# One Strassen level in layer 1 of the last two token groups, with a new instruction order

## The chip, the cores and the metric

The kernel runs on one core of one Trainium2 chip. The metric is the device time of one execution in microseconds; lower is better. Where a kernel was run several times, the median is given. The engines of the core are named as in the profile: PE is the matrix engine (TensorE), PEld its weight loads, DVE is VectorE, ACT is ScalarE, POOL or G is GpSimd, and SP is SyncE, which here only issues DMA transfers.

## The reference

The reference is a linear attention followed by a two-layer network with a gate. In the kernel's terms there are 8 batches of 576 tokens, 8 heads of 64, a model width of 512 and a hidden width of 2048.

```python
def _attn_ref(q, k, v):                      # each (8, 8, 576, 64)
    pos = np.arange(S); theta = np.pi / 2 * pos / S
    phi = lambda x: concat([relu(x) * cos(theta), relu(x) * sin(theta)], -1)
    kv  = einsum('bhsf,bhsd->bhfd', phi(k), v)
    z   = sum(phi(k), axis=2)
    num = einsum('bhsf,bhfd->bhsd', phi(q), kv)
    den = einsum('bhsf,bhf->bhs', phi(q), z)[..., None] + 1e-06
    return num / den

def _moe_ref(x, w_in, w_out):                # x (4608, 512), w_in (512, 2048), w_out (2048, 512)
    h = x @ w_in                             # "layer 1"
    g = h * np.cos(h)                        # the gate
    return g @ w_out                         # "layer 2"
```

The result of the attention, with heads side by side, is `x`.

## The kernel before

The tokens of a batch are split into 4 tiles of 128 tokens and a rest of 64. The four tiles of batch `b` form token group `b` (512 tokens); the rests of all batches form the group `"r"`. The groups are worked on in the order `GO`, and layer 1 of a group is laid beside layer 2 of the one before it.

```python
GO = [0, 1, 2, 3, 4, 5, 6, "r", 7]
STR = set()            # groups whose layer 1 uses a Strassen level: none
AT = {"r", 7}
```

Every piece of work is an operation of a plan: it names the engines that may do it (A for ACT, V for DVE, G for GpSimd), what it depends on and which buffers it takes and frees. A list of numbers, `ORDER`, found by a search outside of the kernel, gives the order in which the operations are emitted and the engine of each (`40A` is operation 40 on ACT). As each engine works through its own instructions in that order, `ORDER` settles everything that happens on it.

The parts of the plan for a batch: loads of k, q, v (SyncE); the features `phi` (ACT, DVE or GpSimd); a copy of v to 16 bit; the transposes of the query features (on PE for batches 0 and 1, by DMA after that); KV products; N products (numerator and denominator); reciprocal and ratio (DVE); the transpose of `x` (on PE for batches 0 to 2, by DMA after that).

```python
def feat(eng, b, name, t, g, hs=ALLH):                    # L201 to L212
    ...
    if eng == "A":
        nc.scalar.activation(out=dst, in_=src, func=AF.Relu, scale=sc)
    else:
        (nc.vector if eng == "V" else nc.gpsimd).tensor_scalar(
            out=dst, in0=src, scalar1=0.0, scalar2=sc, op0=ALU.max, op1=ALU.mult)
...
RING = {"m1": 4, "l2": 2, "at": 1, ..., "qp": 4, "x16": 3, "ch": 3, "g": 2, "s": 3, "ld": 2, "p5": 3, ...}
```

`RING` gives the number of buffers of each kind: `m1`, `l2` and `at` are PSUM, `x16` holds the ratio of a token tile until its transpose has landed.

Layer 1 of a group, plain form: for each of 16 blocks of the hidden width, 4 matmuls of 512 columns into one PSUM buffer, then the sine on ACT and the product with it on DVE.

```python
def moe1(key, g, js, cs, s0, s1):                         # L319 is its matmul
    ...
    for n, j in enumerate(js):
        for c in cs:
            nc.tensor.matmul(ps[key][:, n, :], lhsT=w_in_sb[:, c, j * P:(j + 1) * P],
                             rhs=x[:, c, s0:s1], ...)
def sin(key): ...     # ACT, L381: sin(h + pi/2) from PSUM to "ch"
def gate(eng, key, dst): ...   # DVE: g = h * ch, read from PSUM
```

Layer 2 is in Strassen's form for all groups (seven products X, Y, Z of half-size blocks instead of eight, with sums of `g` and of the weights made on DVE, and additions from PSUM on DVE). The same form for layer 1 stands in the code, but no group uses it as `STR` is empty. Three of the four sums of `w_in` that it needs (`w_in_sum`, tile `WS`) are made all the same.

```python
def quad(g, qd, n):                                       # a quarter of the hidden width, product n of 7
    a11, a12, s3, a22 = (w_in_block(k_, e) for e in range(2) for k_ in range(2))
    ...
    bank, first, lhs, rhs = (
        ("X", True, a11, x_block(g, 0, 0)), ("Z", True, ws[0], xs[0]),
        ("Y", False, ws[1], xs[1]), ("X", False, a12, x_block(g, 1, 0)),
        ("Y", False, s3, x_block(g, 0, 1)), ("Z", False, ws[2], x_block(g, 1, 1)),
        ("Y", False, a22, xs[2]))[n]
    ...
    for i in range(2):
        for c in range(2):                                # 4 matmuls of 256 columns
            nc.tensor.matmul(ps[(g, qd, bank)][:, i, :], lhsT=lhs[:, c, 2 * qd + i, :], rhs=rhs[:, c, :], ...)
...
def quads(g, base, ga):                                   # used for the groups in STR
    for n in range(4): x_sum(...)                         # DVE: sums of x, once a group
    for qd in range(4):
        p1 = mm(0, ...)                                   # X
        p5 = mm(1, ...)                                   # Z
        y1 = op({"A": 0.6, "V": 0.69}, EV, y_seed, deps=[p1, p5], ...)   # copies X into Y
        e5 = op({"A": 0.6, "V": 0.69}, EV, evac5, deps=[p5, ga], ...)    # copies Z out of PSUM
        p6 = mm(2, [xsum[1], wsum1[1], y1], ...)          # onto Y
        p2 = mm(3, [y1], ...)                             # onto X, then sine and gate
        z1 = op({"V": 0.69}, EV, z_add, deps=[p6, e5])    # Z = Y + copy
        p7 = mm(4, [xsum[2], s3_done(), z1], ...)         # onto Y
        c = op({"V": 0.69}, EV, c22, deps=[p7])           # a fourth result, then sine and gate
        p3 = mm(5, [wsum1[2], z1], ...)                   # onto Z, then sine and gate
        p4 = mm(6, [xsum[3], c], ...)                     # onto Y, then sine and gate
...
def cover():                                              # L298: two matmuls of 512 columns with a zero weight
    t = ppool.tile([P, 2, 512], F32, name="cover", tag="at", bufs=1)
    for n in range(2):
        nc.tensor.matmul(t[:, n, :], lhsT=zero, rhs=w_in_sb[:, 0, 0:512], start=True, stop=True)
```

Of the kernel before, what the change touches and what calls it, by code (L numbers as in the profile page):

```python
# [44 lines left out]


ORDER = """
115 22 25 230 180 184 883 818 24 229 342 21 40A 41V 42A 60 43V 44A 61V 62 45A 63V 64 38A 32V 36V
39A 70 37V 31A 34V 51G 53A 54G 52V 35V 50A 4G 30A 33V 5G 46V 57A 71 47V 9G 48A 72V 66 7G 49A 58V
75 56V 85 59A 76V 68 11G 77V 55A 69A 15G 86V 73 87V 78 227 13G 74V 79A 88 89V 90 65A 80 91V 17G  # L50
120 81V 82V 116 19G 67A 92V 95 83 96V 100 84A 97V 93 94V 98 105 101V 99A 117 102V 121 118A 106V
103 132 107V 122A 133 119V 104A 110 134A 136 123V 128 135V 129 124 130A 111V 112V 125 137 126A
131V 140 138A 127V 108 141 109A 139V 113 142A 144 114V 145 143V 152 146A 231 164 147V 153 233
165 154A 168 166A 155V 148 149 167V 176 150A 188V 177 156 151V 178A 199 179V 172 190V 169 189V
160 170A 173 171V 157 174A 161 191V 158A 343 200 162A 159V 236 201A 192V 202 175V 238 163V 203
181V 204A 241 185V 261A 210 182V 263A 211 193V 243 262A 207 186V 246 212A 264V 265A 208 887 248
183V 258A 283 940 209V 254A 281 213V 273G 272A 194V 282A 274G 214 275G 187V 271G 257A 277G 205V
215 259A 279G 251V 280G 217 255A 252V 276G 278G 196V 253A 256A 284V 260A 216V 267A 291 197V 222
292A 269A 305 206V 295 293 266A 296V 218 340 306V 294A 297V 270A 310 195V 285 268A 289 307V 286A
344 223 198V 346 219A 315 891 287 316V 224A 220G 317V 290A 311V 320 349 321V 225G 312V 288A 318  # L60
335 322V 300 419 336V 323 351 319A 301V 308 302V 324A 313 314A 298 309V 303 299V 304A 325 330
326V 819 501 327V 369A 835 331V 328 820 332V 329A 371G 836 821A 370V 831 837A 822V 384 333 832
334A 838V 827 833A 372G 859 354 373V 828 834V 374A 860 843 337V 861A 823 829A 375G 386 844 862V
824 845A 830V 338 825A 356 339V 875 826V 388 376A 876 863 846V 877A 851 361G 368V 390 366A 852
878V 855 853A 856 363V 377A 847 367V 364G 864 857A 362V 848 865A 858V 948 359A 866V 867 849A
365G 854V 839 360A 868 850V 871 869A 884V 840 381A 879 382G 870V 880 841A 379G 885V 958 383A
380G 842V 881A 872 378A 394 886V 420 873A 395 882V 392 949 396A 417 874V 421 397 888V 950A 423
398A 951 889V 399V 952 890V 402 953A 956 426 955V 403A 959 944 404V 957 428 960A 954V 407 1024
961V 405 408A 400 406V 431 962 446A 401V 409V 963 448A 447G 433 412 450A 964V 410 965 449V 413A
411A 414V 451G 970 461 452A 443V 415 453A 971 416V 463 441A 438V 895 439G 442V 444A 440V 465 901  # L70
896A 437V 445V 458A 904 459G 467 897V 457A 966 456G 436V 460A 972V 919 905A 975 967V 902A 973G
471 920A 903V 907 968G 454A 906V 472 908A 455V 928 499 473A 909V 503 474 921V 929A 469 910 475A
930V 922 911A 505 476V 931 923A 912V 477 479 932A 924V 892 480A 933V 916 893A 481V 508 898 917A
894V 482 484 899A 934 918V 485A 900V 925 935A 486V 510 1032 926A 936V 487 489 913 490A 927V 528G
1033 491V 914A 513 937 915V 1034A 492 941V 1035 938A 502 530G 529A 939V 515 494 942V 578 660 543
1036 945V 1040 1037A 532G 946V 524A 1042 522V 525A 1041 1038V 1028 518A 531G 947V 1043 533A 495V
496V 982 534A 1108 1044A 1003 1039V 535G 545 983A 1045V 991 538A 984V 547 542A 976 521V 540G
992A 985 943V 497 536G 977A 993V 1049 549 1004A 539A 1005V 1009 986A 978V 537G 979 1010A 987V
519A 1046 1011V 980A 527V 988 526G 541A 580 981V 1021 989A 582 520V 990V 551 1050 1022A 523G
1023V 997 1051V 1000 998A 999V 994 1052G 1001A 585 1002V 587 1012 995A 996V 1047 1013A 1025V  # L80
605A 1018 590 1048V 607A 606G 1006 1014V 1019A 1054 608V 1007A 1020V 609A 1116 1008V 610A 1015
611V 1026V 1055 1016A 579 592 612A 1017V 1117 1059 1056A 1027V 553 1118A 1057G 1029V 554 1030V
1119 555A 576 596G 599A 1031V 556 1120 620 595A 557V 558V 1124 1121A 597G 1123V 559 598A 561
1126 562V 622 600A 563V 1127 1112 602A 619G 1122V 564 604A 566 616G 1125 567V 624 568V 1128A
617G 601A 1192 615G 1129V 571 569 572A 618A 573V 1130 626 613A 1133 603V 574 614V 630 628 1131
631 662 1132V 1134 632A 658 664 633 1135V 1138 634A 635V 1136G 1096 667 638 1097A 1105 639V 636
640V 1139 1106A 669 1098V 643 641 1140A 1143 1107V 1078 1141G 644V 1066 645V 1079A 687G 1093
1080V 1067A 646 1068V 648 1094A 1060 672 649A 1095V 1072 1061A 689G 650V 688A 1069 1062V 651
1073A 653 1070A 674 1074V 1084 691G 737 690A 702 1071V 1200 654A 1085A 655V 1102 704 679A 680G
1086V 684A 1087 678V 656 1103A 692V 1063 1088A 1104V 706 685G 1090 1064A 1089V 681A 1099 1065V  # L90
1091A 682V 1075 686G 1100A 1092V 677A 1081 1101V 1076A 1165 661 1113V 1082A 683G 1144 1077V
1166A 1114V 699A 1159 698A 1167V 1201 697G 1145A 1083V 693G 700A 1147 1202V 1160A 1109V 1183
1148A 1161V 701A 1203 1110V 1184A 1168 695A 1185V 1208 1149V 696A 1162 1111V 1169A 710 694A
1170V 712 1163A 1146V 708 1153 1164V 713 1154A 739 1115V 1209 714A 735 741 1155V 715 1204 716V
717V 1150 1205A 1206V 718 1210 1151A 1207V 744 720 1196 1152V 1171 746 721V 722V 1180 1172A 1211
1173V 1181A 723 1182V 764A 725 1276 749 1189 726V 1212A 765G 727V 1177 1190A 1213V 728 730 1178A
1156 766V 751 731A 767V 1214 779 1157A 732V 756A 763G 1217 759V 733 758A 1215 762V 781 757A 755V
1218 1216V 754G 761A 1174 1191V 1219A 1158V 760A 1222 1175A 1193V 1220G 1284 775A 1176V 1223
774G 778A 1194V 777A 776G 1186 1227 1195V 1237 768V 1187A 738 1224V 769A 1264 1188V 1225G 1238A
783 789 1179V 1265A 1285 770A 1239V 1231 1286V 771G 1266V 1255 1232A 1197V 1249 1256A 1198V 772G  # L100
785 1228 1250A 1199V 790 1251V 1287 791A 1233V 773A 1267 1257V 1229A 787 1246 1268A 1230V 1258
1247A 1269V 1248V 1270 1259A 1260V 1240 1271A 1272V 1234 1241A 1242V 792 1235A 1288 793V 794V
1273 1289A 1290V 795 1294 1274A 1291V 797 1295 1236V 798A 1275V 1243 799V 1292 1244A 1296V 800
802 1280 1293 803A 1245V 1252 1297V 1360 1277V 1301 1253A 804V 1298 1254V 805 807 1299 808A
1278V 1302 1300V 1279V 1306 1303A 809V 1304G 1368 810 1307 812 1308V 1311 1369 813A 1309G 814V
1261 1370A 815 1371 1262A 1263V 1376 1281V 1372 1282V 1423 1373A 1374V 1377 1283V 1411 1375V
1378 1327 1364 1336 1328A 1329V 1379 1337A 1338V 1342 1380A 1444 1381V 1318 1343A 1344V 1385
1319A 1320V 1348 1354 1349A 1350V 1386 1355A 1356V 1330 1387A 1388G 1324 1331A 1332V 1382 1325A
1326V 1315 1312 1316A 1317V 1383 1313A 1314V 1321 1384V 1452 1322A 1323V 1390 1357 1351 1358A
1359V 1391 1352A 1353V 1402 1395 1412A 1392V 1424A 1417 1413V 1403A 1393G 1453 1404V 1418A 1426  # L110
1454A 1419V 1425V 1339 1427A 1428V 1429 1340A 1341V 1333 1430A 1431V 1441 1334A 1335V 1396 1442A
1443V 1455 1397A 1361V 1414 1398V 1345 1415A 1362V 1405 1346A 1416V 1347V 1460 1406A 1363V 1456
1407V 1420 1457A 1458V 1399 1421A 1365V 1422V 1432 1400A 1401V 1462 1433A 1366V 1438 1448 1367V
1461 1439A 1459V 1463 1440V 1408 1464V 1465V 1435 1409A 1410V 1469 1436A 1445V 1466 1437V 1489
1446V 1467 1447V 1470 1468V 1434V 1474 1471A 1449V 1472G 1479 1450V 1475 1451V 1480 1476A 1477G
1490 1481V 1487 1491A 1482 1488 1483 1492V 1493 1485V 1484V 1496 1486V 1494 1497 1495V 1501
1498V 1502 1499 1506 1503A 1507 1504 817 1508A 1505 1509 1510
"""


@with_exitstack
def kernel(
    ctx: ExitStack,
    tc: tile.TileContext,
    q: bass.AP,
    k: bass.AP,
# [557 lines left out]

    GO = [0, 1, 2, 3, 4, 5, 6, "r", 7]
    ALONE = (1, 7)
    STR = set()
    AT = {"r", 7}
    WSUM = {"Vp": 1.24}
    XSUM = {"Vp": 0.43}  # L690
# [37 lines left out]
    def layer1(g, base, after):  # L728
# [3 lines left out]
        gate_ops[g] = {}  # L732
        if g in STR:
            quads(g, base, ga)
# [258 lines left out]
```

## Time and profile before

| | |
|---|---|
| time, median of 3 runs | 313.49 us (312.3 to 313.61) |
| span of the profiled run | 310.2 us |
| DMA | 53.30 MB, mean 172 GB/s |
| granted PE clock, mean | 0.987 |

The costliest groups of instructions on the page (busy us, and the mean of one):

| what | count | busy us | mean ns |
|---|---|---|---|
| PE, layer 1 (L319, xT) | 640 | 122.3 | 338 |
| ACT, sines (L381) | 144 | 84.3 | 596 |
| DVE, gates (L332, g) | 128 | 84.8 | 685 |
| GpSimd, features of q (L211) | 20 | 42.0 | 2106 |
| ACT, features of q (L209) | 44 | 29.9 | 713 |
| DVE, ratio (L276) | 44 | 26.2 | 594 |

How to read it: a line of code can be that of a helper which records many kinds of work, so groups are told apart by their tiles. M is a PSUM tile of layer 1, PX, SD and PZ are those of layer 2, `ch` is the sine, `N` the attention's numerator and denominator. Matmuls overlap, and so do instructions of DVE and ACT that follow each other; the mean of one is longer than the step from one to the next. The chain of waits is followed back from the last instruction, each step to what released it.

### The profile page before, as it was taken

The numbers are of one execution on the slowest core, as the hardware profiler recorded it, in microseconds if no ns is written. First come the engines' busy times: TensorE is split into PE (matmuls) and PEld (weight loads), VectorE is DVE, ScalarE is ACT, GpSimd is POOL, SyncE is SP. The second block draws the span as 40 slices with busy tenths as digits, with TensorE's granted clock in tenths as the row PEclk, the third lists the DMA queues.
The fourth block names the chain that finished last, engine by engine and source line by source line (L and its number), as shares of the span: only waits on it lengthen the run. The fifth ranks groups of instructions, "written<-read, shape, count | busy, mean of one in ns | idle before, by whom it ended". The sixth has DMA issues, their size and how long they took to land.

```text
span 310.2 us, 6724 instructions
## 1 busy us (share of the span) xinstructions
PE 281.8 (91%) x2615; PEld 205.1 (66%) x2615; DVE 233.6 (75%) x440; ACT 180.3 (58%) x326; POOL 111.7 (36%) x114
## 2 busy tenths in 40 slices
PE   8758958889999998999987699999999999999993
PEld 8647837768887556558863346675578766566882
DVE  1867767979988888888844698898887665788741
ACT  2776428988847857867726388586731254654200
POOL 1270004058708329983714990276001101100220
PEclk9999979999999999999999799999999999999999
DMA  7799993099899999899899983999314401100123
GB/s 220 244 145 200 209 343 109 0 288 288 155 266 279 232 278 256 172 257 357 149 161 312 294 118 59 264 294 215 70 34 73 117 2 68 68 2 0 50 87 136
DMA packets 77247, 53.30 MB, mean 172 GB/s; under 512 B 46112, under 2 KB 74784, under 8 KB 77216
## 3 DMA queue, kind: packets, MB, share of 16 engines
q1 hardware_dynamic: 69920, 39.86, 53.3%
q0 software_dynamic: 6848, 12.59, 16.0%
q8 instruction: 20, 0.33, 0.5%
q10 hardware_dynamic: 448, 0.44, 0.4%
q14 instruction: 11, 0.09, 0.1%
HBM read 36.74 MB, written 9.44 MB: 149 GB/s over the span
## 4 chain that ended last, share of the span: by engine, by line
PE 60%; DMA 20%; ACT 6%; DVE 3%; issue 1%; SPq 1%; POOL 0%; ACTq 0%; DVEq 0%
PE M L319 29%; PE SD L430 11%; PE PX L430 9%; DMA xT<-x 9%; DMA w_out_sb<-in_moe_w_out_dram 7%; PE PZ L430 7%; PE KV L247 3%; ACT kp L209 3%; DMA km<-in_k_dram 2%; DMA qm<-in_q_dram 2%; PE N L256 1%; ACT qp L209 1%; DVE g L332 1%; DVE x L276 1%; ACT ch L381 1%
## 5 line engine op out<-in xcount | busy, mean ns | idle before, releaser
L319 PE MATMUL M<-xT,w_in_sb 128*128 128x512 f16 (+1 forms) x640 | 122.3, 338 | 6.0 <-DMA xT<-x 1.8
L381 ACT ACTIVATE ch<-M 128x512 f32<-128x512 f32 x144 | 84.3, 596 | 57.0 <-PE M L319 55.4
L319 PEld LDWEIGHTS <-w_in_sb 128*128 128x128 f16 x704 | 67.2, 98 | 52.5 <-issue 5.3
L332 DVE TENSOR_TENSOR g<-M,ch 128x512 f16<-128x512 f32 x128 | 84.8, 685 | 14.2 <-ACT ch L381 12.8
L430 PEld LDWEIGHTS <-g 128*128 128x128 f16 x640 | 61.9, 99 | 20.4 <-issue 7.3
L211 POOL TENSOR_SCALAR qp<-qm,CS 128x512 f16<-128x512 f32 x20 | 42.0, 2106 | 40.7 <-DMA qm<-in_q_dram 22.8
L430 PE MATMUL PX<-w_out_sb,g 128*128 128x256 f16 x256 | 34.4, 280 | 4.1 <-DMA w_out_sb<-in_moe_w_out_dram 3.0
L465 POOL DMA_DIRECT2D out_dram<-ost x14 | 7.8, 560 | 76.2 <-ACT ost L189 55.2
L209 ACT ACTIVATE qp<-qm,CS 128x512 f16<-128x512 f32 x44 | 29.9, 713 | 6.9 <-DMA qm<-in_q_dram 6.9
L276 DVE TENSOR_TENSOR x<-N,rec 128x512 f16<-128x512 f32 (+1 forms) x44 | 26.2, 594 | 8.6 <-DMA xT<-x 6.4
L211 POOL TENSOR_SCALAR kp<-km,CS 128x512 f16<-128x512 f32 x14 | 29.3, 2105 | 3.1 <-DMA km<-in_k_dram 2.7
L430 PEld LDWEIGHTS <-s 128*128 128x128 f16 x256 | 24.5, 98 | 4.7 <-issue 0.2
L209 ACT ACTIVATE kp<-km,CS 128x512 f16<-128x512 f32 x37 | 24.5, 711 | 2.5 <-DMA km<-in_k_dram 2.5
L191 POOL CAST V<-vm 128x512 f16<-128x512 f32 (+1 forms) x24 | 12.6, 563 | 28.3 <-DMA vm<-in_v_dram 27.8
L332 DVE TENSOR_TENSOR gr<-M,ch 128x512 f16<-128x512 f32 x16 | 11.1, 692 | 10.2 <-ACT ch L381 10.2
L211 DVE TENSOR_SCALAR kp<-km,CS 128x512 f16<-128x512 f32 x29 | 16.3, 597 | 2.1 <-DMA km<-in_k_dram 2.1
L430 PE MATMUL PZ<-w_out_sb,g 128*128 128x256 f16 x128 | 16.6, 273 | 0.0
L430 PE MATMUL PZ<-WT,s 128*128 128x256 f16 x128 | 16.3, 273 | 0.0
L319 PE MATMUL M<-xR,w_in_sb 128*128 128x512 f16 x64 | 15.5, 379 | 0.0
L430 PE MATMUL SD<-WT,g 128*128 128x256 f16 x112 | 14.5, 273 | 0.7 <-ACT ost L189 0.7
L256 PEld LDWEIGHTS <-qT 128*128 128x128 f16 x256 | 12.5, 98 | 3.8 <-issue 0.9
L256 PE MATMUL N<-kvz,qT 128*128 128x65 f16 x256 | 14.1, 194 | 1.0 <-DVE x L276 0.9
(91 smaller groups left out, 312.2 us busy)
## 6 DMA issues: line engine op xcount, KB each, us to landing
out_dram<-ost POOLq DMA_DIRECT2D x28, 256.0 KB, 4.5
qm<-in_q_dram SPq DMA_DIRECT2D x8, 640.0 KB, 5.5
km<-in_k_dram SPq DMA_DIRECT2D x8, 640.0 KB, 8.0
qm<-in_q_dram SPq DMA_DIRECT2D x8, 512.0 KB, 6.0
km<-in_k_dram SPq DMA_DIRECT2D x8, 512.0 KB, 8.4
vm<-in_v_dram SPq DMA_DIRECT2D x6, 640.0 KB, 6.7
vm<-in_v_dram SPq DMA_DIRECT2D x6, 512.0 KB, 6.2
w_in_sb<-in_moe_w_in_dram POOLq DMA_DIRECT2D x4, 512.0 KB, 9.1
```

The lines of the kernel that those rows point to most:

```text
L191: (nc.vector if eng == "V" else nc.gpsimd).tensor_copy(out=out, in_=in_)
L209: nc.scalar.activation(out=dst, in_=src, func=AF.Relu, scale=sc)
L211: (nc.vector if eng == "V" else nc.gpsimd).tensor_scalar(out=dst, in0=src, scalar1=0.0, scalar2=sc, op0=ALU.max, op1=ALU.mult)
L247: nc.tensor.matmul(tile_[:, n, hh, :], lhsT=kps[b][:, t, h].rearrange("p g d -> p (g d)"), rhs=V1[:, t, h, :], start=(t == 0), stop=(t == NT))
L256: nc.tensor.matmul(tile_[:, n, hh, :], lhsT=qT(p, t)[:, h, :], rhs=kvzs[p][:, h, :], start=(i == 0), stop=(i == len(parts) - 1))
L276: nc.vector.tensor_tensor(out=dst, in0=tile_[:, :, :, 0:D], in1=rec.unsqueeze(3).broadcast_to((P, nb, HB, D)), op=ALU.mult)
L319: nc.tensor.matmul(ps[key][:, n, :], lhsT=w_in_sb[:, c, j * P:(j + 1) * P], rhs=x[:, c, s0:s1], start=(c == 0 and n == 0), stop=(c == NCT ...
L332: (nc.vector if eng == "V" else nc.gpsimd).tensor_tensor(out=out, in0=in0, in1=in1, op=op)
L381: nc.scalar.activation(out=ps[("ch", key)], in_=ps[key].rearrange("p j s -> p (j s)"), func=AF.Sin, bias=math.pi / 2.0, scale=1.0)
L430: nc.tensor.matmul(ps[(g, bank)][:, i, :], lhsT=lhs[:, j, i * P:(i + 1) * P], rhs=rhs[:, c * HJ // 2 + j], start=(first and i == 0 and j = ...
L465: e0.dma_start(out=five[:, t0:t0 + 2, :], in_=blocks(ost, n))
```

## The change

Layer 1 of the groups `"r"` and 7, the last two, takes the Strassen form that stands in the code. This is to save one of eight products in the part of the kernel in which PE has hardly a pause. With it comes another searched order for the whole kernel; as the Strassen form adds operations, the numbers in the two lists stand for different operations from that part on, and other operations go to other engines too. In neither order does GpSimd run an operation with two inputs; it copies, makes features and issues DMA transfers.

```diff
@@ ORDER @@
-115 22 25 230 180 184 883 818 24 229 342 21 40A 41V 42A 60 43V 44A 61V 62 45A 63V 64 38A 32V 36V
... (all lines of the list are replaced)
+180 24 184 22 25 230 229 342 883 115 818 21 40V 42V 41A 43V 44A 60 62 61V 46A 63V 48A 32V 37A
...
     GO = [0, 1, 2, 3, 4, 5, 6, "r", 7]
     ALONE = (1, 7)
-    STR = set()
+    STR = {"r", 7}
     AT = {"r", 7}
```

What the new order holds, counted by kind:

| operations | before | after |
|---|---|---|
| plain products of layer 1 on PE / with sine and gate | 176 / 144 | 144 / 112 |
| Strassen products of layer 1 on PE / sines and gates of them | 0 / 0 | 56 / 32 |
| seeds of Y and copies of Z in layer 1 (ACT, DVE) | 0, 0 | 15, 1 |
| z additions and c22 additions in layer 1 (DVE) | 0 | 16 |
| sums of x, fourth sum of w_in (DVE) | 0, 0 | 8, 1 |
| features of q on ACT, DVE, GpSimd | 44, 16, 20 | 35, 24, 21 |
| features of k on ACT, DVE, GpSimd | 37, 29, 14 | 38, 29, 13 |
| copies of layer 2's results and seeds on ACT, DVE | 30, 14 | 41, 3 |

The "cover" matmuls stand at the end of PE's sequence before, and ahead of the second Strassen product of group `"r"` after. The transposes of `x` of batch 5 stand among the loads of batch 6 in SyncE's sequence, before as "load q, load q, load k, transpose 0, load k, transpose 1, transpose 2", after as "load q, load q, transpose 0, load k, transpose 1, load k, transpose 2". The first features of query 2 on ACT and DVE stand before the first sine and gate of group 1 before, and behind the first ones after.

## The prediction

> **What bounds the kernel now.** I read the busy shares of the page first, then the busy time by stretch, then the chain of waits, and last the waits of single stretches. The busy shares (engine, busy us, share of the span, instructions) make TensorE (PE) the engine to look at, with VectorE (DVE) second.
>
> ```profile
> PE 281.8 (91%) x2615; PEld 205.1 (66%) x2615; DVE 233.6 (75%) x440; ACT 180.3 (58%) x326; POOL 111.7 (36%) x114
> ```
>
> An average hides the stages, so the next view is busy time by stretch. Columns: stretch and its length, then busy us and instruction count of PE, weight loads, DVE, ACT and POOL, then the granted PE clock, the share of the DMA engines and GB/s.
>
> ```profile
> 0.00:43.00 43.00, 32.47 (x397) 28.52 (x398) 26.33 (x66) 23.04 (x41) 9.08 (x22) 1.00 0.98 216
> 43.00:72.00 29.00, 24.85 (x289) 20.47 (x287) 24.93 (x58) 22.53 (x41) 9.58 (x16) 0.94 0.54 180
> 72.00:147.00 75.00, 72.99 (x694) 52.65 (x693) 66.30 (x118) 54.63 (x102) 45.68 (x32) 1.00 1.03 249
> 147.00:177.00 30.00, 23.64 (x245) 16.77 (x243) 17.78 (x39) 14.50 (x29) 16.66 (x15) 0.94 0.97 226
> 177.00:240.00 63.00, 62.56 (x538) 41.82 (x537) 54.57 (x96) 39.78 (x72) 22.98 (x18) 1.00 0.64 144
> 240.00:305.00 65.00, 64.34 (x457) 44.50 (x456) 43.74 (x68) 25.40 (x44) 7.66 (x14) 1.00 0.16 50
> ```
>
> The reader is to see two kinds of stage. In 72–147 and from 177 on PE is busy 97 to 99%: there a microsecond of PE work less is a microsecond less, unless the products begin to wait. In 0–72 and in 147–177 PE has holes, and the clock column falls to 0.94 in two of these stretches. The chain of waits (start, length, what) says what the holes are:
>
> ```profile
> 20.63 22.09 DMA w_out_sb<-in_moe_w_out_dram
> ...
> 61.85 5.71 DMA qm<-in_q_dram
> 67.67 0.72 ACT qp L209
> 68.66 0.97 ACT ch L381 x2
> ...
> 162.75 9.69 DMA xT<-x
> 172.57 0.70 DVE x L276
> 173.31 1.06 PE N L256 x16
> ```
>
> So until 42.8 us the second weight matrix is awaited. Near 62–68 ACT stands at a feature of batch 2 whose query load has not landed. At 162.75 a DMA transpose of x (batch 5, token tile 0) is issued and lands 9.7 us later; the normalised tile that reuses its buffer waits for it, and PE waits for that:
>
> ```profile
> PE N L256 <- DVE x L276: 5.2, 2, 4.7
> ```
>
> **What the Trainium skill says.** "TensorE: Matmul & The Clock Gate", section "Back-to-back issue gap", gives N/2.4 + 2.5 ns for a warm matmul of N columns: 216 ns at 512 and 109 ns at 256. The trace agrees: four 512-column matmuls take 0.86 us in the chain, eight of 256 columns 0.87. The same page, "What's actually happening", has the array drop to half clock after about 3.4 us of idleness and recover after a busy window of about that length. The trace agrees here too: a wait of 3.00 us before 42.8 and one of 4.75 us before 173.3 are each followed by 3.4 us at clock 0.5, which costs about 1.7 us more. "VectorE: DVE Perf Modes", "The perf-mode tier table", caps tensor_tensor at double rate for 16-bit SBUF operands and at single rate with PSUM: the trace has 0.68–0.69 us both for 1024 fp16 elements and for 512 elements read from PSUM. "DMA: Bandwidth & Descriptors", "Queues, rings and completion order", says that on each DMA engine the descriptors of one ring are consumed in ring order; the 9.69 us transpose, issued behind 1.8 MB of loads from the same SyncE queue, fits.
>
> **The change, part by part.**
>
> (a) Layer 1 of the groups r and 7. Before, each needs 16 x 4 matmuls of 512 columns: 64 x 0.216 = 13.8 us. After, each needs 4 quads x 7 products x 4 matmuls of 256 columns: 112 x 0.109 = 12.2 us. Saved: 1.6 us a group, 3.3 us in all. Weight loads rise from 64 to 112 a group at 98 ns; that is under the 109 ns of a 256-column matmul, as layer 2 has it already without a visible loss. Both groups are in the last stage, where PE is 99% busy, so this counts in full if nothing new waits.
>
> (b) The two "cover" matmuls of 512 columns, 0.43 us, stood behind the last product (305.35 us, beside the last output copy, which cost nothing). They now stand ahead of the second product of group r: plus 0.4 us. Net on PE: about -2.9 us.
>
> (c) DVE in the last stage. New there: 8 z additions and 8 c22 additions (0.69–0.70 us each, as the like additions of layer 2), one evacuation 0.69, the fourth sum of w_in 1.2 (like its three sisters at 1.22), and 8 sums of x of 512 fp16 elements, which I estimate at 0.4 from the 0.68 of 1024 elements. That is 11.7 + 1.2 + 3.2 = 16.1 us; three copies of layer 2 go from DVE to ACT, -2.1. The 32 gates are the same in number and size. DVE goes from 43.7 to about 58 us of busy time in some 62. That looks full, but busy times overlap: gates that follow each other start 0.60–0.61 us apart though each is 0.69 long, so 58 busy is about 51 of engine time, 82%.
>
> (d) ACT in that stage. 8 seeds of Y and 7 evacuations at 0.60, plus 1.8 for the copies from DVE: 25.4 + 10.8 = 36 us of 62. No bound.
>
> (e) Chains. In a quad the first product must pass through ACT (seed), product 6, DVE (z), product 7, DVE (c22) before product 4: about 0.6 + 0.7 + 0.7 on the engines, three products of 0.435 and the hand-overs, some 4.5 us. The new PE order puts two to three quads and products of layer 2 between, so each quad has about 7 us of other PE work around it. I allow 0.7 us for stalls. Tail: -2.2 us.
>
> (f) The searched order elsewhere. PE's own sequence before group r is nearly the same. Three places differ where the trace shows a wait. First, at 62–68 us ACT and DVE stood at features of query 2 ahead of a copy of x and ahead of the first gates of group 1; these features now come after several sines and gates, and the third one went to GpSimd, which is idle there. PE had about 2.7 us of holes in 60–70; I count -1. Second, near 160 SyncE issued two query loads and a key load ahead of the transpose that landed after 9.7 us; now two query loads alone, 1.15 instead of 1.8 MB. At the 226 GB/s of that stretch the missing 0.64 MB are 2.8 us, and ten instead of nine products of PE stand between the five N blocks of batch 5. The wait of 4.75 us could shrink to about 1 and its half-clock window go. Against that, ACT now has the features of query 6 after four sines of group 4 instead of after six, and the last query feature of batch 5, which frees the buffer for that load, is late on GpSimd (2.1 us each there, against 0.71 on ACT). I count -2, not -5. Third, new places where an in-order queue stands at a late load must be expected in an order whose search knew no real landing times: +1.
>
> Sum: 313.5 - 2.2 - 1 - 2 + 1 = 309.3; I say **309.5**.
>
> **Rivals.** *DVE becomes the bound of the tail.* For it: DVE gets the largest share of the new work, and a z addition behind a gate that waits for a sine holds up two products. Against it: 18% of engine time is left, and DVE already sits idle there for 10.2 us of group r's gates, waiting for sines. It would eat the 3.3 us and perhaps 3 more: 313 to 317. *The gain is given back in the middle.* The order before 240 us is a different one, and a single new wait of over 3 us at a load costs that and a half-clock window: 312 to 316. *The middle heals wholly.* If the wait before 173 and its clock window both go, 4.75 + 1.7 us come on top of the tail: 303 to 305. *Nothing early can change:* until 42.8 us the landing of the weights decides, and the loads are issued in the same manner; I hold this for very likely.
>
> **Range and chances.** The tail is -2.2 with about 1.5 of doubt, the middle -2 with about 4. That makes 304 to 316 for 8 in 10. Faster by 2% means under 307.2: it needs the middle to heal nearly wholly, 0.30. Slower by 2% means over 319.8: two rivals at once, 0.06. Within 2%: 0.64.
>
> **What would show it.** Right: PE's instruction count up by some 96 less a few records, its busy share at 98% or more from the first x sum to the last product, the stretch from P6's first product to the end about 2–3 us shorter, DVE about 10–15 us busier in all; the transpose of x of batch 5 landing in under 8 us. Wrong in (e): waits of PE in the last stage for z additions, seeds or gates. Wrong in (f): the clock column of the middle still under 1.00, or a new line of PE waiting for a DMA or for a feature. Prediction wrong as a whole: a time over 316, or the tail not shorter at all while the middle is what moves the time.

## The result and the profile after

The changed kernel takes 309.01 us (median of 4 executions, 307.88 to 309.41), beside 313.53 us (312.3 to 313.61) for the kernel before on the same chip: a ratio of 0.986, with a 95% interval of 0.982 to 0.990. The prediction of 309.5 us holds. The rest of this document asks whether it holds for its reasons; in part it does not.

The busy shares of the kernel after (engine, busy us, share, instructions):

```profile
PE 279.3 (91%) x2711; PEld 215.7 (71%) x2711; DVE 248.9 (81%) x463; ACT 187.9 (61%) x342; POOL 115.7 (38%) x116
```

PE has 96 instructions more and 2.5 busy us less; DVE has 15 us more. Busy time by stretch of the kernel after, in the columns of the prediction:

```profile
0.00:43.00 43.00, 34.19 (x401) 30.23 (x402) 26.94 (x68) 22.08 (x40) 9.07 (x22) 0.96 0.98 223
43.00:72.00 29.00, 25.52 (x310) 22.06 (x310) 27.48 (x62) 25.12 (x45) 13.66 (x17) 1.00 0.66 207
72.00:147.00 75.00, 71.66 (x680) 51.61 (x678) 66.71 (x117) 52.56 (x96) 49.76 (x35) 1.00 1.00 236
147.00:177.00 30.00, 27.80 (x253) 17.72 (x251) 24.60 (x48) 18.17 (x35) 17.61 (x13) 0.94 1.04 219
177.00:236.00 59.00, 57.41 (x514) 39.32 (x514) 50.26 (x88) 35.49 (x68) 17.92 (x17) 1.00 0.64 164
236.00:301.00 65.00, 62.51 (x563) 54.75 (x560) 52.90 (x86) 34.07 (x61) 7.67 (x14) 1.00 0.12 45
```

In 147–177 PE is busy 27.80 us instead of 23.64. In the last row DVE has 52.90 of 65 us, ACT 34.07: neither is full. But PE, with less to do there, also falls from 99% to 96%. From the chain of waits of the kernel after (start, length, what):

```profile
20.26 21.37 DMA w_out_sb<-in_moe_w_out_dram
...
85.68 9.30 DMA km<-in_k_dram
95.83 2.10 DVE kp L215 x3
...
150.52 2.48 DMA xT<-x
```

The load of w_out still decides until 41.6 us, as expected. The transpose of 9.69 us is no longer in the chain. A key load of 9.30 us, with the features on DVE behind it, is new there. PE's waits of the kernel after in 147–180:

```profile
PE N L260 <- DMA xT<-x: 1.4, 1, 1.4
PE N L260 <- DVE x L280: 0.8, 2, 0.6
```

The 4.7 us before the last N block of batch 5 are gone.

**Two marks in the trace.** Executions of these kernels spread over several microseconds, so I cut the trace at operations that every version has and compare pieces. The last piece, the *tail*, runs from the first `PZ<-w_out_sb,g` behind 215 us (a Z product of layer 2 of group 5) to the start of the last run of twelve `SD<-WT,g` matmuls (Y products of layer 2 of group 7). In PE's timeline of the kernel before:

```profile
232.90 1.03 PE L430 MATMUL PZ<-w_out_sb,g 128*128 128x256 f16 x8
...
302.79 1.47 PE L430 MATMUL SD<-WT,g 128*128 128x256 f16 x12
```

and in that of the kernel after:

```profile
229.77 1.04 PE L434 MATMUL PZ<-w_out_sb,g 128*128 128x256 f16 x8
...
298.52 1.47 PE L434 MATMUL SD<-WT,g 128*128 128x256 f16 x12
```

So the tail takes 69.89 us before and 68.75 after, and the *head* ahead of it 232.90 and 229.77. The two tails do not hold the same work, however: before, 24 N matmuls of batch 7 come behind the mark (0.26 and 0.48 us of PE's timeline, at 234.64 and 239.34), after, all of them come ahead of it. Of the 4.3 us between the last marks, the Strassen form thus brings about 0.4 and the new order of the head about 3.9. The head is cut further: *early*, up to the first N product behind 140 us (146.52 and 145.20); *middle*, from there to the first `SD<-WT,g` product behind 200 us (207.68 and 205.37); *late*, the rest. As the two orders put different work between these inner marks, they are compared only among versions with the same order of the head.

### The profile page after: what moved, and what is told of

Same layout as the page of the kernel before. It is cut to its first block, busy times and chain, and to the rows that moved or that the text cites. A ratio compares the mean times of both kernels' runs of the same rounds, so it can differ in the third digit from the quotient of the medians.

```text
span 305.8 us, 6944 instructions
## 1 busy us (share of the span) xinstructions
PE 279.3 (91%) x2711; PEld 215.7 (71%) x2711; DVE 248.9 (81%) x463; ACT 187.9 (61%) x342; POOL 115.7 (38%) x116
## 4 chain that ended last, share of the span: by engine, by line
PE 55%; DMA 15%; DVE 15%; ACT 3%; POOL 2%; issue 2%; SPq 1%; ACTq 0%; DVEq 0%; POOLq 0%
PE M L323 20%; PE SD L434 10%; DMA w_out_sb<-in_moe_w_out_dram 7%; PE PX L434 7%; PE PZ L434 6%; DMA km<-in_k_dram 6%; DVE g L336 5%; PE M L379 3%; DVE kp L215 3%; PE YZ L379 3%; PE KV L251 2%; DMA xT<-x 2%; PE N L260 2%; PE SD L379 2%; ACT ch L385 1%
## 5 line engine op out<-in xcount | busy, mean ns | idle before, releaser
L323 PE MATMUL M<-xT,w_in_sb 128*128 128x512 f16 (+1 forms) x576 | 106.0, 334 | 5.2 <-DMA xT<-x 1.5
L385 ACT ACTIVATE ch<-M 128x512 f32<-128x512 f32 x124 | 72.2, 596 | 35.2 <-PE M L323 28.3
L336 DVE TENSOR_TENSOR g<-M,ch 128x512 f16<-128x512 f32 x118 | 77.4, 684 | 10.7 <-ACT ch L385 10.3
L323 PEld LDWEIGHTS <-w_in_sb 128*128 128x128 f16 x576 | 54.9, 98 | 40.0 <-issue 4.2
L215 POOL TENSOR_SCALAR qp<-qm,CS 128x512 f16<-128x512 f32 x21 | 44.2, 2109 | 29.9 <-DMA qm<-in_q_dram 29.4
L213 ACT ACTIVATE qp<-qm,CS 128x512 f16<-128x512 f32 x35 | 24.0, 717 | 7.8 <-DMA qm<-in_q_dram 5.9
L213 ACT ACTIVATE kp<-km,CS 128x512 f16<-128x512 f32 x38 | 25.5, 712 | 4.8 <-DMA km<-in_k_dram 4.8
L195 POOL CAST V<-vm 128x512 f16<-128x512 f32 (+1 forms) x26 | 16.4, 664 | 29.3 <-DMA vm<-in_v_dram 29.2
L215 DVE TENSOR_SCALAR kp<-km,CS 128x512 f16<-128x512 f32 x29 | 18.9, 683 | 3.9 <-DMA km<-in_k_dram 3.9
L215 DVE TENSOR_SCALAR qp<-qm,CS 128x512 f16<-128x512 f32 x24 | 13.1, 566 | 5.2 <-DMA qm<-in_q_dram 5.2
L434 PE MATMUL SD<-w_out_sb,g 128*128 128x256 f16 x112 | 15.8, 291 | 0.0
```

Source lines behind the costliest of these rows:

```text
L195: (nc.vector if eng == "V" else nc.gpsimd).tensor_copy(out=out, in_=in_)
L215: (nc.vector if eng == "V" else nc.gpsimd).tensor_scalar(out=dst, in0=src, scalar1=0.0, scalar2=sc, op0=ALU.max, op1=ALU.mult)
L336: (nc.vector if eng == "V" else nc.gpsimd).tensor_tensor(out=out, in0=in0, in1=in1, op=op)
L385: nc.scalar.activation(out=ps[("ch", key)], in_=ps[key].rearrange("p j s -> p (j s)"), func=AF.Sin, bias=math.pi / 2.0, scale=1.0)
L434: nc.tensor.matmul(ps[(g, bank)][:, i, :], lhsT=lhs[:, j, i * P:(i + 1) * P], rhs=rhs[:, c * HJ // 2 + j], start=(first and i == 0 and j = ...
```

## The experiments

Entries of `ORDER` are named by their numbers; a number without a letter is an operation of PE or SyncE. Medians are of all executions of a kernel. The ratio to the kernel before on the same chip leaves out executions over 1.5% above their kernel's fastest, 40 of the 59 of the kernel before on the chip of e5 among them, so it is not always the quotient of the medians.

**Head or tail? (e1, e2)**

```diff
 # e1: order of before up to the first layer 2 product of group 6, then that of after
-    STR = set()
+    STR = {"r", 7}
```

> The order of before up to the first layer-2 product of group 6, and from there the tail of after with the Strassen form of layer 1 in r and 7. Theory T, from the two traces: nearly all of the 4.5 us came from the part ahead of the tail, and the tail saves 3.3 us of products but loses about 2.4 us in new waits and 0.4 in the cover matmuls; so this is 313.0 us (312.3 to 313.8). The prediction on record (tail -2.2, middle -2): 311.3 us. If all of the gain is the tail's: 309.

```diff
 # e2: order of after up to the same place, then that of before
-    STR = {"r", 7}
+    STR = set()
```

> The order of after up to the first layer-2 product of group 6, and from there the tail of before, with layer 1 plain in all groups. Theory T: 309.5 us (308.8 to 310.5), as the head alone brings about 3.9 us. The prediction on record: 311.5 us. If all of the gain is the tail's: 313.5. With e1, the gains of head and tail should add up to that of after within 1 us.

e1: 317.68 us, ratio 1.014 (1.010 to 1.019). It can't answer the question, since joining two orders made waits of its own. PE's timeline of e1:

```profile
173.03 1.06 PE L257 MATMUL N<-kvz,qR 128*128 128x65 f16 x16 [4.69 <-DVE x L277]
...
243.50 0.61 PE L299 MATMUL cover<-w_in_sb,zero 128*128 128x512 f16 x2 [0.83 <-DVE w_in_sb L333]
...
246.40 0.60 PE L376 MATMUL M<-xsr,WS 128*128 128x256 f16 x4 [2.29 <-DVE xsr L333]
```

The first line is useful: the wait of the kernel before at 173 us is there again with the head of before (4.75 there, 4.69 here). The last two are the joint: the sums of `x` of group r need a transpose that in the order of before is issued just ahead of them.

e2: 314.97 us, ratio 1.006 (1.003 to 1.009). Its tail takes 69.99 us; the kernel after, with the same order of the head, has 68.75. But not all of these 1.24 us are the Strassen form's, as e2 has a joint too, with a wait that neither before nor after has:

```profile
243.69 1.03 PE L427 MATMUL PX<-w_out_sb,g 128*128 128x256 f16 x8 [0.67 <-ACT SD L186]
```

The eight matmuls ahead of it start at 241.98, and eight such matmuls that follow each other start 0.87 us apart, so this costs 0.84 us. Without it the tail of e2 is 69.15 us. The tail of before without its 24 N matmuls, 69.89 - 0.74, is 69.15 too. So the Strassen form saves about 0.4 us in the kernel after.

The head of e2 takes 234.9 us, though it is the order that took 229.8 in the profile after. PE's timeline of e2 shows one reason:

```profile
99.05 3.42 PE L316 MATMUL M<-xT,w_in_sb 128*128 128x512 f16 x9 [3.10 <-DVE xT L188]
```

and DVE's timeline of e2 what held the copy:

```profile
94.96 1.32 DVE L208 TENSOR_SCALAR qp<-qm,CS 128x512 f16<-128x512 f32 x2 [1.44 <-DMA qm<-in_q_dram]
98.17 0.49 DVE L208 TENSOR_SCALAR kp<-km,CS 128x512 f16<-128x512 f32 x1 [1.90 <-DMA km<-in_k_dram]
98.57 0.42 DVE L188 COPY xT<-TP 128x512 f16<-128x512 f16 x1
```

DVE stands at two features whose loads have not landed, and behind them is the copy of `x` that layer 1 of group 2 needs. The kernel after has the same wait at 95.9 us, 1.0 us long, as its loads landed earlier.

**The transposes of batch 5 alone (e4, e10, e6)**

```diff
 # e4 and e10: the kernel before with two key loads issued one transpose later
- 667 638 ... 636 640V ... 1106A 669 1098V ... 641 1140A
+ 638 ... 636 667 640V ... 1106A 1098V ... 641 669 1140A     # 667, 669: loads of k; 636, 641: transposes of x
```

> Before, with SyncE's transposes of x of batch 5 (tiles 0 and 1) each put ahead of the key load of batch 6 that preceded it, as after has it; nothing else. Theory T: 0.64 MB less is queued ahead of the transpose that landed after 9.7 us, so it lands after some 7 us; PE's wait of 4.75 us shrinks to about 2 and its half-clock window goes: 313.5 - 2.8 - 1.7 = 309 us at best, 311 if the window stays. Rival, the wait is of the products before it and the loads only move: 313.5.

> e4 once more: the order of before with the two transposes earlier, layer 1 plain everywhere. On the chip of e1 to e4 it was 4.9 us under before. If that holds it is 308 to 309 us here. It is the base for e11.

```diff
 # e6: the kernel after with the same two pairs the other way round
- 1140A 636 1141G ... 667 640V ... 1088A 641 1089V ... 669 1090
+ 1140A 1141G ... 667 636 640V ... 1088A 1089V ... 669 641 1090
```

> After, with SyncE's two transposes of x of batch 5 put back behind the key loads of batch 6, as before has them; nothing else. Theory T2, that this detail makes most of the gain: the wait of PE before the last N block of batch 5 and the wait of DVE for the transpose come back, 3 to 5 us slower than after: 312.5 to 314. Rival, the rest of the order makes the gain: 309 to 310.

e4: 307.86 us, ratio 0.984 (0.980 to 0.988). e10, the same kernel on another chip: 308.86, ratio 0.987 (0.983 to 0.992). Two entries of the list, and nothing of Strassen, bring as much as the whole change. e6: 315.18, ratio 1.018 (1.010 to 1.026), 3.2 us over the kernel after on that chip (e5, below). PE's waits in 147–180 of e10:

```profile
PE M L316 <- DVE g L329: 1.7, 1, 1.7
PE M L316 <- issue: 1.5, 1, 1.5
PE N L253 <- DVE x L273: 0.4, 1, 0.4
```

and the place in PE's timeline of e6:

```profile
169.85 0.72 PE L257 MATMUL N<-kvz,qR 128*128 128x65 f16 x16 [3.09 <-DVE x L277]
```

The wait of 3.09 us before the last N block (the one of 16 matmuls) of batch 5 is the one that before has with 4.75. In e10 that block does not wait: its line of 0.4 us is of another block. Two other waits, of 1.7 and 1.5 us, stand in this stretch of e10. SyncE's timeline shows the issue, of the kernel before:

```profile
159.94 1.27 SPq L201 DMA_DIRECT2D qm<-in_q_dram  x1
...
162.02 0.63 SPq L201 DMA_DIRECT2D km<-in_k_dram  x1
162.75 1.99 SPq L680 DMA_TRANSPOSE xT<-x  x1
```

of the kernel after:

```profile
158.52 0.61 SPq L205 DMA_DIRECT2D qm<-in_q_dram  x1
...
160.38 1.20 SPq L684 DMA_TRANSPOSE xT<-x  x1
161.68 0.61 SPq L205 DMA_DIRECT2D km<-in_k_dram  x1
```

and of e6:

```profile
159.66 0.66 SPq L202 DMA_DIRECT2D km<-in_k_dram  x1
160.41 1.73 SPq L681 DMA_TRANSPOSE xT<-x  x1
```

The transpose goes out 2.4 us earlier after than before, but 1.4 of that is the whole sequence, as its first query load goes out earlier by as much; the change of place is worth about 1 us of issue. The larger part is the landing: this first transpose of batch 5 lands 9.7 us after its issue in the kernel before, 6.1 after. The kernel after and e6 issue it at the same time, 160.38 and 160.41, and in e6, with the key load ahead, it lands 8.6 us later. The Trainium skill ("DMA: Bandwidth & Descriptors", "Queues, rings and completion order") says that each DMA engine takes the descriptors of one ring in ring order; these times agree with it and add the size.

**The kernel after once more (e5).** Unchanged, with 22 executions beside 59 of the kernel before, on another chip.

> The changed kernel itself once more, beside the next three on one chip, as the kernels with its head (e2, e3) spread from 308 to 316 us. Theory T2: the head of after has waits at loads whose length differs from execution to execution (near 96 us and near 160 us), so it spreads more than e4; median 309.5 (308 to 312). Rival: the spread of e2 and e3 came from their edits; then 309.0 with all runs within 1 us.

312.02 us (307.6 to 315.1), beside 312.67 (307.5 to 316.5): ratio 0.998 (0.993 to 1.003). The gain of the first measurement is not there. The tail of e5 is again 68.75 us; the head takes 236.9. (Its profiled execution took 315.0 us, that of e6 311.1, and that of the first measurement 307.9.)

The pieces of all traces, in us (e3, e7 to e9, e11 and e12 follow below), with the time from issue to landing of the first transpose of `x` of batch 5, and PE's wait before the last N block of that batch. "Loads" are the two key loads of batch 6:

| order of the head | trace | early | middle | late | tail | landing | wait |
|---|---|---|---|---|---|---|---|
| before | before | 146.5 | 61.2 | 25.2 | 69.89 | 9.7 | 4.8 |
| before | e1 | 146.0 | 62.8 | 25.5 | with the joint | 9.3 | 4.7 |
| before, loads later | e4 | 144.6 | 58.4 | 24.9 | 69.89 | 6.8 | 1.0 |
| before, loads later | e10 | 147.0 | 57.5 | 25.3 | 69.89 | 6.4 | 0 |
| before, loads later | e7 | 144.6 | 58.6 | 26.4 | 70.92 | 7.8 | 1.0 |
| before, loads later | e8 | 144.7 | 58.5 | 25.9 | 70.14 | 7.6 | 1.9 |
| before, loads later | e11 | 146.9 | 58.3 | 25.5 | 69.04 | 7.6 | 0.6 |
| before, loads later | e12 | 147.9 | 58.6 | 25.3 | 69.05 | 7.4 | 1.6 |
| after | after | 145.2 | 60.2 | 24.4 | 68.75 | 6.1 | 0 |
| after | e2 | 148.5 | 62.0 | 24.4 | 69.99 | 5.7 | 0 |
| after | e3 | 149.2 | 62.6 | 24.4 | 67.98 | 7.0 | 1.4 |
| after | e5 | 150.1 | 62.4 | 24.4 | 68.75 | 7.1 | 2.5 |
| after | e9 | 148.1 | 61.5 | 24.4 | 68.74 | 6.2 | 1.6 |
| after, loads sooner | e6 | 144.9 | 63.7 | 24.4 | 68.74 | 8.6 | 3.1 |

Four readings. The tail of one order is the same in every execution to 0.01 us. The landing takes 8.6 to 9.7 us in the three traces with a key load ahead, and 5.7 to 7.8 in the other eleven; the waits are 3.1 to 4.8 and 0 to 2.5. The middle tells the two versions of the load order apart in every trace: 61.2 and 62.8 against 57.5 to 58.6 with the order of before, 63.7 against 60.2 to 62.6 with that of after. The early piece moves by 2.4 us with the order of before (without e12) and by 5.2 with that of after (without e9), though nothing in it was changed; the recorded profile of the kernel after has nearly the shortest.

**The stalls in the tail (e3, e7, e8, e11).** PE's waits of the kernel after in 236–302:

```profile
PE YZ L379 <- ACT ch L385: 1.1, 2, 0.6
PE YZ L379 <- DVE gr L336: 0.8, 1, 0.8
PE SD L434 <- ACT ost L193: 0.6, 1, 0.6
```

The kernel before has only the last of these. One of the three new ones in PE's timeline of the kernel after, and ahead of it what DVE and ACT did:

```profile
275.65 0.69 DVE L336 TENSOR_TENSOR p<-YZ,p 128x512 f32<-128x512 f32 x1 [0.17 <-PE YZ L379]
276.37 0.60 ACT L385 ACTIVATE ch<-YZ 128x512 f32<-128x512 f32 x1 [1.28 <-DVE p L336]
```

```profile
277.02 0.60 PE L379 MATMUL YZ<-xs,w_in_sb 128*128 128x256 f16 x4 [0.46 <-ACT ch L385]
```

The product adds onto Y, whose last reader, the c22 addition, ended at 276.34. It starts at 277.02, when the sine of Z ended (276.97). In these quads Y and Z are halves of one PSUM tile, and the product waits for the reader of the other half. The three products stand 0.82, 0.46 and 0.60 us at such a wait; from start to start they come 0.99, 0.62 and 0.76 us late, 2.4 in all. In each case the c22 addition was done when PE came to the product or 0.02 us later (248.70, 276.34 and 288.39, beside 249.12, 276.40 and 288.37), so the data of Y itself did not hold it. e3 puts the last product of the three quads concerned one PE operation later, so that the wait falls beside other work:

```diff
 # e3: the kernel after; the last products of three quads (1352, 1468, 1506) behind the next product of layer 2
- 1352 1397 ... 1412        - 1468 1534        - 1506 1546A ... 1554
+ 1397 ... 1412 1352        + 1534 1468        + 1546A ... 1554 1506
```

> After, with the last product of three quads whose Y and Z lie in one PSUM tile (r quad 1, 7 quads 1 and 3) put behind the product of layer 2 that followed it. Theory T: these products wait for readers of the other half of the tile (0.82, 0.46 and 0.60 us of idle PE) and not for data, so PE work in between hides the wait: 1.5 us less than after, 307.5. Rival, the tail is held by DVE as a whole: the waits turn up at the next products and nothing is gained, 309.

311.25 us (three executions at 308.2 to 309.0, three at 313.5 to 314.1), ratio 0.987 (0.983 to 0.991). The total says little, but the tail falls by 0.77 us, to 67.98, and of these waits in 242–308 of e3 there is left

```profile
PE YZ L376 <- DVE g L333: 0.5, 1, 0.5
```

The move brings back only 0.77 of the 2.4 us: the last of the three still comes 0.62 us late, and smaller delays turn up at other products, one of them a wait of 0.3 us for a copy on DVE. The Strassen form can thus save 1.2 us of the tail (69.15, as above, to 67.98). The same three moves were then put on the better head of e4.

```diff
 # e7: head of e4, tail of after; 1393 and the rest of batch 7 (804V, 805, 807 ...) moved up, against the joint of e1
-    STR = set()
+    STR = {"r", 7}
 # e8: e7 and the three moves of e3
 # e11: e8 with layer 2 of group 5 ahead of batch 7, and product 1506 one PE operation later still
- 804V 805 ... 1297V 1393 ... 1298 1254V 1261 ...
+ 1297V 804V 805 1393 ... 1298 ... 1254V 1299 1300V ...     # 1297V: z addition, 1298, 1299: products, 1300V: c22 addition
```

> e4 (the order of before with the two transposes earlier) up to the first layer-2 product of group 6, then the tail of after with the Strassen form in r and 7; unlike e1, the last N blocks of batch 7 and the last plain product of group 6 are put 3 to 6 products earlier, so that the sums of x and of w_in find their data. Against e4 this shows what the tail of after is worth by itself. Theory T: 3.3 us of products less, 0.4 for cover and 2.4 of waits more: 0.5 us under e4, 307.4. The prediction on record (tail -2.2): 305.7. Rival, DVE bounds the tail: 309 or more.

> e7 with the last product of the three quads with a common tile for Y and Z one place later, as in e3. The trace of e3 showed two of the three waits gone and 0.45 us still there in the last one: 0.8 to 1.5 us under e7, 306.3; the fastest of all if the theory of the common tile holds. Rival: the same as e7.

> e8 with the seam between the two orders mended: the trace of e8 shows PE waiting 0.75 us for a z addition and 1.27 us for a c22 addition of group 5, both behind other DVE work that the seam had put ahead; now they come first. Also the last product of the last quad one more place later. Theory T: 2 us less than e8, 307, and 1.5 us less than e10, as the tail with Strassen then saves 3.3 us of products and loses only cover (0.4) and about 1.4 of waits. Rival, Strassen in the tail is worth nothing whatever the order: equal to e10.

e7: 310.13 us, ratio 0.998 (0.994 to 1.002); e8: 309.17, 0.997 (0.993 to 1.001), both with 22 executions on the chip of e5. The tail goes from 70.92 to 70.14: again 0.78 us for the three moves. It is longer than that of e4 all the same, as the joint has waits for the z and c22 additions of group 5. The second falls into the tail: PE stands 1.27 us, and the products come 1.44 us late. Without that, e7 is 0.4 us shorter than e4 in the tail and e8 1.2, as found above. e11, with these mended: tail 69.04, 308.70 us, ratio 0.986 (0.981 to 0.991), beside e10 with 69.89 and 308.86 on the same chip. So with the same head the Strassen form brings 0.85 us in the traces, and the total times cannot tell the two apart. It is not 1.2, as product 1506 no longer waits but the layer-2 product that now comes ahead of it waits 0.7 us for ACT. Busy time of e11 in the last stretch:

```profile
236.00:301.00 65.00, 63.88 (x574) 55.89 (x573) 55.31 (x90) 34.18 (x61) 8.80 (x16) 1.00 0.14 52
```

PE is at 98% here, with DVE at 55.31.

**The copy behind the features (e9)**

```diff
 # e9: the kernel after; three features of batch 3 on DVE (449V, 450V, 442V) behind the copy of x of batch 2 (416V)
- 449V 970 967A 450V 461 968G 442V ... 416V 439A
+ 970 967A 461 968G ... 416V 449V 450V 442V 439A
```

> After, with DVE's copy of the last transposed x tile of batch 2 put ahead of three features of batch 3 (q, q, k) that wait for their loads; nothing else. In two executions of after PE waited 1.01 and 3.77 us for this copy, while DVE stood at those features. Theory T2: this is one of the two places where the new order stands at a load, and most of its spread: the wait goes, median 1.5 to 3 us under e5, 309 to 310.5. Rival: the features are needed soon after and the wait moves on to the gates; then as e5, 312.

312.26 us, ratio 0.998 (0.994 to 1.002): no gain to be seen over e5. The wait for the copy is gone, and another stands in its place. PE's timeline of e9:

```profile
101.45 4.44 PE L320 MATMUL M<-xT,w_in_sb 128*128 128x512 f16 x12 [2.63 <-DVE g L333]
```

The gates are now behind the features: DVE works on features from 94.69 to 100.72 us, with only 0.75 us at a load, and the gate that PE needs comes after them. To move one operation past the features moved the wait on to the next one.

**The features of query 2 (e12)**

```diff
 # e12: e11; query feature 369 on GpSimd instead of ACT, 370V and the transposes that need it (384) behind a gate (834V)
- 369A 835 ... 821A 370V 831 ... 822V 384 ... 834V 374A
+ 369G 835 ... 821A 831 ... 822V ... 834V 370V 384 374A
```

> e11 with the first query features of batch 2 as after has them: one on GpSimd instead of ACT, one on DVE behind three gates of group 1 instead of ahead of them. The prediction counted 1 us for this; in the trace of before PE had 2.7 us of holes there but most of them are the transposes of x: 0 to 1 us less than e11.

308.85 us, ratio 0.989 (0.985 to 0.994), beside 308.70 of e11; the early piece is 147.9 against 146.9. ACT no longer waits 1.1 us for the query, but then waits 1.5 us for the transposes on PE: nothing is gained.

## Why the prediction was right, and where it was not

**(a), (b) Products and cover.** Right. PE has 96 instructions more. By their starts in the timelines, four matmuls of 512 columns take 0.86 to 0.87 us and four of 256 columns 0.43 to 0.44, which is 3.3 us less over both groups, and cover takes 0.43.

**(c), (d) DVE and ACT.** Right, and the rival of a full DVE falls: the three waits of PE in the tail are for a shared tile and not for an engine without time, since moving three products takes 0.77 us of them away with DVE's work unchanged, and in e11 PE reaches 98% beside 55.3 us of DVE. DVE was reckoned at 58 us of some 62; the last row of the kernel after has 52.9 of 65. A sum of `x`, estimated at 0.4, takes 0.42 us.

**(e) Stalls.** The mis-sized term. The prediction allowed 0.7; the tail shows 3.3 - 0.4 - 0.4 = 2.5 us, of which 2.4 are the three late products. It counted the chain of a quad, which does fit between the others, and not that a product also waits for the readers of the other half of its tile. The tail therefore gave about 0.4 us instead of 2.2. Its signs said so: PE is at 96% in the last stage and not at 98, and it waits there for sines and gates.

**(f) Query 2: -1.** Not found (e12): ACT's wait for the query goes, another takes its place, and the time stays.

**(f) Transposes: -2.** The mechanism holds, by doing it alone (e4, e10) and by undoing it (e6). The prediction reckoned with the bytes ahead in the queue, 2.8 us of them, and with a landing in under 8 us; it went from 9.7 to 6.1. Only the size was too small: the times move by 4.9, 3.4 and 3.2 us (the last between two kernels that spread over 5 and more), and the middle is 2.6 to 5.3 us shorter with the order of before, 1.1 to 3.5 with that of after. Two signs of being wrong came up without meaning it: a new line of PE waiting for a transpose (1.4 us), and the clock column of the middle, still at 0.94, but for another half-clock window, at 153 us. In e4, where nothing else was changed, the column is at 1.00: there the window went with the wait, as forecast.

**(f) New waits: +1.** Right that they would come, too small. In the profile after they are modest (1.0 us for the copy at 95.9). In e2, e3, e5 and e9, which share that head but for the moves of e9, it ended at 234.0 to 236.9 us instead of 229.8. That is as late as the head of before (232.9; 234.3 in e1), so what the transposes brought is given back, as the second rival had it. In which piece, the marks cannot say across the two orders; among the traces with the order of after, the early piece is 145.2 to 150.1 us and the middle 60.2 to 62.6.

So the total was right in the first measurement by luck as much as by reason, through terms of which one was too large (tail), one too small (transposes) and one not constant (new waits). On the chip of e5, the order of after is worth 0.2% (with an interval that holds zero); on that of e9, the same order with e9's move as little. What is sure of the change is the tail's 0.4 us of 313, or 0.1%.

**What stays open.** Why loads land some microseconds sooner in one execution than in another, from the first piece on, was not tried. Nor was a Strassen form with Y and Z in two tiles, which would test the shared tile directly, or a head that keeps the loads of batch 3 away from DVE's copies and gates altogether. No version clearly beats the kernel before with two entries moved.

## What to carry to other kernels

Where executions of a kernel differ by more than a change can bring, cut the trace at marks that both versions have: a tail that repeats to 0.01 us tells 0.8 us apart which no median here could. But count the work between the marks, and look for waits of the joint, before a difference is called a saving: of the 1.24 us between e2 and the kernel after, 0.84 were a wait of e2's joint. In an in-order DMA queue, issue the small transfer that frees a buffer ahead of the bulk loads that nobody waits for yet; here that alone was worth as much as a new order of all instructions. Before counting an eighth of the products as saved, look at which results share a PSUM tile: here a product then waited for the readers of its neighbour, and that took 2.4 of 2.9 us.

## What the hardware showed unexpectedly

In these traces half-clock windows (stretches at a granted clock of 0.5) do not follow the length of a wait alone. The kernel after has one at 153.1 us, with no longer wait than 1.4 us, though PE was busy for only 2.0 of the 4 us ahead of it; e6 has one behind a wait of 3.09 us; e5 has none behind one of 3.77 us at 100.4. In the kernel before, the wait of 3.00 us at 42.8, behind which one follows, is shorter than the 3.4 us of idleness that the prediction names. The Trainium skill ("TensorE: Matmul & The Clock Gate", "What's actually happening") calls the window of the activity monitor free-running, so that the moment of a change depends on where in it the first matmul falls. That the same holds for a wait would fit, but no trace here shows where a window begins.
